# A fused attention and gated feed-forward kernel on one Trainium2 core: a second norm without its scaled sums, one more pair-added score half, and a new order

## The chip, the cores and the metric

The kernel runs on one core of one Trainium2 chip. The metric is the device time of one execution in microseconds (us), as the median of several runs. The engines of the core are named as in the profile: PE (matrix products), PEld (its weight loads), DVE (vector), ACT (scalar), POOL and SP, which here mostly issue DMAs.

## The reference, cut to what matters

x has 2048 rows of 512 numbers in bf16. H = 32 heads of 16 numbers; every position attends to W = 8 earlier positions, 2 apart.

```python
def _layernorm(x, eps=1e-5):
    return (x - mean(x)) / sqrt(var(x) + eps)

def _A_ref(x, wqkv, wo):                     # sliding, dilated attention
    q, k, v = split(x @ wqkv)                # 32 heads of 16
    idx = pos[:, None] - arange(8) * 2       # eight positions back, two apart
    logits = einsum("bhsd,bhswd->bhsw", q, k[idx]) * 16 ** -0.5   # masked where idx < 0
    return einsum("bhsw,bhswd->bhsd", softmax(logits), v[idx]) @ wo

def _B_ref(x, W_gate, W_up, W_down):         # 512 -> 1376 -> 512
    return (relu(x @ W_gate) * (x @ W_up)) @ W_down

h  = x + _A_ref(_layernorm(x), A_wqkv, A_wo)
h2 = h + _B_ref(_layernorm(h), B_W_gate, B_W_up, B_W_down)
```

The second norm is what the change touches first. The kernel does not divide h - mean by its standard deviation ahead of the two products: relu(a g) (a u) = a² relu(g) u for a positive a, so the rows go in centred only, and the factor 1 / (var + eps) is put on the output of the down product.

## The kernel before, in words

The rows are worked in four chunks of 512 (written tk, or "/0" to "/3" below), each of four blocks j of 128 rows. For a chunk: first norm (`xst`, `xag`, `xxn`), transposes (`xtp`), twelve q, k and v products of four matmuls each (`qkv`, for chunk 0's first six cut in parts `qka` to `qke`), and their copies out of PSUM on ACT (`qe`). The scores: for each half hf of the eight offsets DVE multiplies q by shifted k (`pr0`, `pr1`: two instructions of 128x4096 for a half, L638), PE sums over the 16 numbers of a head with a 0/1 matrix of 32 columns (`sc0`, `sc1`, L644), ACT takes exp (`ex`), DVE normalises (`es`, `am`), SP spreads each row over four partitions by DMA (`bd0S`, `bd1S`, L763), DVE multiplies by shifted v (`mu`, L795) and adds the eight products (`tree`, L798 and L832), where the first of three additions is an accumulating DMA that POOL issues (`ta`, L838). Then the output product (`wo`, L876), the residual sum on DVE (`rs`, L887), which also gives each row's sum `sm`, the second norm, transposes on PE (`htp`, chunk 0) or by DMA from SP (`htd`, L535, the other chunks), gate and up products (`mm`, L949; the last 96 of the 1376 columns as `mm5`, L916), copies and relu on ACT (`ue`, `ge`), the product gate times up on DVE (`gu`, L977, and `gu5`, L926), and the down product (`dn`, L1000) with its output step (`o`, `os`).

The second norm of a block before the change: DVE scales the row sum, mv = -sm / 512 (`hnm`, L452); ACT sums the squares of x + mv (`hsq`, L458); ACT makes 1 / (var + eps) as exp(-ln(...)) (`hrl`, `hre`, L479 and L486); DVE writes the centred rows x + mv (`hxn`, L512).

For chunk 3 both halves of the scores are pair-added: with (tk, hf) in `PRE`, DVE adds the second product tile to the first (`pa`, L682, one instruction of 128x4096), and PE sums 8 tiles instead of 16 (L689).

The order is no hand-written loop. Every step is an operation with an engine, a duration, dependences and buffers, and the list `RANK` gives each its place. `Plan.order` walks the operations strictly in the order of `RANK`, sets each at the earliest time its own cost table allows, and issues them in the order of these times. So every engine has one fixed sequence, and an engine waits at the first instruction whose input is not there.

At the start, SP and ACT issue the loads of x and of the four slices of the q and k weights (`wqk_sb`, L324 from ACT for slices 0 to 2, L339 from SP for slice 3). Parts `qka` and `qkd` of the first products need slices 0 and 1, part `qkb` needs slices 2 and 3.

Of the kernel before, what the change touches and what calls it, by code (L numbers as in the profile page):

```python
# [8 lines left out]
P = 128  # L9
BF16 = mybir.dt.bfloat16  # L10
F32 = mybir.dt.float32
I32 = mybir.dt.int32
ACT = mybir.ActivationFunctionType
# [188 lines left out]
def kernel(  # L202
# [11 lines left out]
    nc = tc.nc  # L214
# [11 lines left out]
    PRE = ((3,0),(3,1))  # L226
# [31 lines left out]
    eps_t = sb.tile([P, 1], F32, name="eps_t")  # L258
# [57 lines left out]
    def setup():  # L316
# [11 lines left out]
        nc.gpsimd.memset(eps_t[:], EPS)  # L328
# [108 lines left out]
    def layernorm(tk, src, dst_slots, pr, groups, on_act, residual=None):  # L437
# [7 lines left out]
        for grp in groups:  # L445
            ag, nms = [], {}
            gk = str(grp[0]) if len(groups) > 1 else ""
            lo, hi = grp[0], grp[-1] + 1
            for j in grp:
                if residual:  # L450
                    def f_nm(j=j):
                        V.tensor_scalar(out=mv.t[:, j, 0:1], in0=sm.t[:, j:j + 1], scalar1=-1.0 / D,  # L452
                                        scalar2=None, op0=ALU.mult)

                    h = src[j][1] if tk in RPE else None

                    def f_sq(j=j, h=h):
                        nc.scalar.activation(out=junk[:, j % 2, :], in_=h.t[:] if h else x_sm[:, tk * BPC + j, :],  # L458
                                             func=ACT.Square,
                                             bias=mv.t[:, j, 0:1], scale=1.0, accum_out=sq.t[:, j:j + 1])  # L460

                    a = nms[j] = add((ln + "nm" + gk, tk), "DVE", DSM, f_nm, [src[j][0]], pr, take=[mv], use=[sm], lat=DL)
                    ag.append(add((ln + "sq" + gk, tk), "ACT", 0.66 if h else 0.72, f_sq, [a], pr,
                                  take=[sq], use=[mv] + ([h] if h else []), lat=AL))
# [12 lines left out]
            def f_ln(lo=lo, hi=hi, sq=sq):  # L477
                if residual:
                    nc.scalar.activation(out=rs.t[:, lo:hi], in_=sq.t[:, lo:hi], func=ACT.Ln,  # L479
                                         bias=eps_t[:, 0:1], scale=1.0 / D)  # L480
                else:
                    nc.scalar.activation(out=rs.t[:, lo:hi], in_=mv.t[:, lo:hi, 1], func=ACT.Ln,
                                         bias=eps_t[:, 0:1], scale=1.0 / D if sq else 1.0)
# [23 lines left out]
            def f_xn(j, xn):  # L507
                x = x_sm[:, tk * BPC + j, :]
                if residual and on_act:
                    nc.scalar.activation(out=xn.t[:], in_=x, func=ACT.Identity, bias=mv.t[:, j, 0:1], scale=1.0)  # L510
                elif residual:
                    V.tensor_scalar(out=xn.t[:], in0=x, scalar1=mv.t[:, j, 0:1], scalar2=None, op0=ALU.add)  # L512
# [577 lines left out]
```

## Time and profile before

| | us |
|---|---|
| median of 3 runs | 192.77 (192.36 to 194.35) |
| the profiled execution | 193.22 |
| span of its trace, first to last instruction | 191.3 |
| PE busy, of the span | 185.3 (97%) |
| DVE busy | 149.6 (78%) |
| ACT busy | 115.2 (60%) |
| granted PE clock | 0.997 |

The span leaves out 1.9 us of the execution's own time. In the views below a row of a timeline begins with its start from the span's first instruction and its length, both in us; "x8" is a count, "A<-B" is output from input, and a bracket tells how long the engine sat idle ahead of it and what ended that. A row of a group of instructions ends with busy us, the mean ns of one, and the idle us in front of them.

### The profile page before, as it was taken

Reading aid. Unit: us, or ns where it says so; the run is one execution under the profiler, and the core shown is the slowest. Engines: PE = TensorE matmul, PEld = TensorE weight load, DVE = VectorE, ACT = ScalarE, POOL = GpSimd, SP = SyncE. Lnnn points to the kernel's source line nnn. Section 1 sums busy time; section 2 is a strip of 40 time slices with the busy share of each in tenths; the row PEclk is TensorE's granted clock in tenths of the full one; section 3 lists DMA queues with packets and bytes.
Section 4 is the critical chain, followed back from the end, with each engine's and each line's share of the span. In section 5 each row is a group of like instructions: output and inputs, shape, how many; then the busy total and the mean of one; then the engine's idle time right before and its main releaser. Section 6 shows DMA issues by size and latency. Waiting matters only on the chain.

```text
span 191.3 us, 3033 instructions
## 1 busy us (share of the span) xinstructions
PE 185.3 (97%) x1101; PEld 96.5 (50%) x1120; DVE 149.6 (78%) x246; ACT 115.2 (60%) x236; POOL 18.5 (10%) x34
## 2 busy tenths in 40 slices
PE   7899999999999999999999999999999999999993
PEld 7795555544455444644445544444446444445452
DVE  6899999999999999999999987999627503212632
ACT  2589999976748967753454875144855528517500
POOL 3000002500000042000055000042100000000000
PEclk9999999999999999999999999999999999999998
DMA  5998464992068589993479916779900460120302
GB/s 159 331 351 327 102 157 84 200 196 45 0 258 228 168 154 193 183 279 61 88 131 186 203 33 139 164 151 186 211 4 0 82 165 0 31 82 0 82 25 88
DMA packets 26718, 26.44 MB, mean 138 GB/s; under 512 B 12528, under 2 KB 22608, under 8 KB 26704
## 3 DMA queue, kind: packets, MB, share of 16 engines
q1 hardware_dynamic: 23248, 16.39, 30.9%
q0 software_dynamic: 2736, 8.91, 25.1%
q10 hardware_dynamic: 720, 0.95, 1.5%
q8 instruction: 9, 0.15, 0.3%
q14 instruction: 5, 0.04, 0.1%
HBM read 8.42 MB, written 2.10 MB: 55 GB/s over the span
## 4 chain that ended last, share of the span: by engine, by line
PE 94%; DMA 3%; issue 1%; ACTq 0%; DVE 0%
PE bank L949 36%; PE bank L587 22%; PE bank L1000 20%; PE bank L876 7%; DMA wqk_sb<-in_A_wqkv_dram 3%; PE bank L644 3%; PE bank L916 3%; PE bank L546 2%; PE bank L689 1%; PE bank L720 0%; ACTq L324 0%; ACTq L322 0%; DVE row L1008 0%
## 5 line engine op out<-in xcount | busy, mean ns | idle before, releaser
L949 PE MATMUL bank<-quad,wgu_sb 128*128 128x512 bf16 x311 | 72.1, 379 | 0.4
L949 PEld LDWEIGHTS <-wgu_sb 128*128 128x128 bf16 x320 | 30.9, 98 | 36.9 <-issue 1.7
L1000 PE MATMUL bank<-wd_sb,gT 128*128 128x512 bf16 (+3 forms) x195 | 39.6, 355 | 0.2
L956 ACT ACTIVATE gr<-bank 128x512 bf16<-128x512 f32 x40 | 23.2, 607 | 17.0 <-PE bank L949 13.0
L977 DVE TENSOR_TENSOR gT<-gr,up_sb 128x1024 bf16<-128x1024 bf16 x20 | 13.7, 688 | 23.5 <-ACT up_sb L953 20.3
L587 PE MATMUL bank<-quad,wqk_sb 128*128 128x512 bf16 (+2 forms) x171 | 30.0, 319 | 1.0 <-DMA wqk_sb<-in_A_wqkv_dram 0.7
L953 ACT CAST up_sb<-bank 128x512 bf16<-128x512 f32 x40 | 22.6, 594 | 10.5 <-PE bank L949 8.5
L1000 PEld LDWEIGHTS <-gT 128*128 128x128 bf16 (+1 forms) x198 | 18.5, 98 | 19.9
L638 DVE TENSOR_TENSOR big<-quad,kT 128x4096 bf16<-128x4096 bf16 x11 | 24.9, 2283 | 0.0
L587 PEld LDWEIGHTS <-wqk_sb 128*128 128x128 bf16 x176 | 16.9, 114 | 11.2 <-DMA wqk_sb<-in_A_wqkv_dram 0.9
L795 DVE TENSOR_TENSOR big<-big,vT 128x4096 bf16<-128x4096 bf16 x9 | 20.2, 2282 | 0.0
L458 ACT ACTIVATE junk<-x_sm,mv 128x512 bf16<-128x512 bf16 x16 | 11.7, 730 | 10.0 <-DVE mv L452 9.9
L587 PE MATMUL bank<-quad,wv_sb 128*128 128x512 bf16 x63 | 15.6, 379 | 0.1
L876 PE MATMUL bank<-wo_sb,quad 128*128 128x512 bf16 x63 | 15.2, 379 | 0.1
L838 POOL DMA_DIRECT2D big<-big x12 | 11.2, 1018 | 38.5 <-PE bank L587 29.4
L887 DVE SCALAR_TENSOR_TENSOR x_sm<-x_sm,bank 128x512 bf16<-128x512 bf16 x16 | 10.5, 680 | 3.7 <-PE bank L876 3.7
L798 DVE TENSOR_TENSOR big<-big 128x1024 bf16<-128x1024 bf16 (+2 forms) x18 | 11.5, 655 | 0.1
L1008 DVE SCALAR_TENSOR_TENSOR row<-bank,iv,x_sm 128x512 bf16<-128x512 f32 (+2 forms) x10 | 6.2, 640 | 6.8 <-PE bank L1000 6.8
L469 DVE BATCH_NORM_STATS2 st<-x_sm 128x6 f32<-128x512 bf16 x16 | 10.3, 681 | 1.2 <-DMA x_sm<-in_A_x_dram 1.2
L595 ACT CAST kT<-bank 128x512 bf16<-128x512 f32 x16 | 9.1, 592 | 2.8 <-DVE big L638 2.8
L595 ACT CAST quad<-bank 128x512 bf16<-128x512 f32 x16 | 9.4, 596 | 2.1 <-PE bank L587 1.9
L595 ACT CAST vT<-bank 128x512 bf16<-128x512 f32 x16 | 9.4, 596 | 2.0 <-PE bank L587 2.0
(79 smaller groups left out, 173.7 us busy)
## 6 DMA issues: line engine op xcount, KB each, us to landing
big<-big POOLq DMA_DIRECT2D x12, 512.0 KB, 5.7
big<-ex SPq DMA_DIRECT2D x32, 128.0 KB, 2.7
wqk_sb<-wqk_sb POOLq DMA_DIRECT2D x3, 512.0 KB, 4.5
wgu_sb<-in_B_W_gate_dram SPq DMA_DIRECT2D x1, 1376.0 KB, 11.2
wgu_sb<-in_B_W_up_dram SPq DMA_DIRECT2D x2, 688.0 KB, 4.7
wd_sb<-in_B_W_down_dram SPq DMA_DIRECT2D x2, 640.0 KB, 5.2
x_sm<-in_A_x_dram SPq DMA_DIRECT2D x2, 512.0 KB, 7.2
x_sm<-up_sb POOLq DMA_DIRECT2D x4, 256.0 KB, 5.1
```

Source lines behind the costliest of these rows:

```text
L458: nc.scalar.activation(out=junk[:, j % 2, :], in_=h.t[:] if h else x_sm[:, tk * BPC + j, :], func=ACT.Square, bias=mv.t[:, j, 0:1], scale= ...
L587: nc.tensor.matmul(mm.t[:, lo:hi], lhsT=wv_sb[:, dt, t:D:NT] if c == 2 else wqk_sb[:, dt, c * D + t:(c + 1) * D:NT], rhs=xnT.t[:, dt, lo:h ...
L595: nc.scalar.copy(out=o, in_=mm.t[:])
L638: V.tensor_tensor(out=pb.t[:].rearrange("p (t w) s -> p t w s", t=2), in0=q4, in1=k4, op=ALU.mult)
L795: V.tensor_tensor(out=mt.t[:], in0=ab.t[:], in1=v8, op=ALU.mult)
L798: V.tensor_tensor(out=mt.t[:, 0:n, :], in0=mt.t[:, 0:n, :], in1=mt.t[:, n:2 * n, :], op=ALU.add)
L876: nc.tensor.matmul(od.t[:], lhsT=OT.t[:, t, j * P:(j + 1) * P], rhs=wo_sb[:, t, :], start=(t == 0), stop=(t == NT - 1 and tk not in RPE))
L949: nc.tensor.matmul(mm.t[:fs, lo:hi], lhsT=wgu_sb[:, dt, g, ft * P: ft * P + fs], rhs=hnT.t[:, dt, lo:hi], start=(dt == 0), stop=(dt == NT ...
L953: nc.scalar.copy(out=ub.t[:fs, i, :], in_=um.t[:fs, :])
L956: nc.scalar.activation(out=gr.t[:fs, i, :], in_=gm.t[:fs, :], func=ACT.Relu)
L977: V.tensor_tensor(out=gt.t[:fs, 0:n, :], in0=gr.t[:fs, 0:n, :], in1=ub.t[:fs, 0:n, :], op=ALU.mult)
L1000: nc.tensor.matmul(od.t[:, c0:c1], lhsT=gts[ft].t[:fs, ft % 2, j * P:(j + 1) * P], rhs=wd_sb[:fs, ft, c0:c1], start=(ft == 0), stop=(ft == ...
```

## The change

The second norm works without `hnm`: instead of x - sum/512 it takes 512 x - sum, so the sum is used as it is. Squares, variance and centred rows grow by 512 or its square, and eps with them; the factor on the output divides it out. The pair addition is extended to the second half of chunk 2, `(2,1)`. `RANK` is a new list of 745 places in place of 760. `PRE2` is empty, so the branch for it makes nothing.

```diff
 RANK = [
...
-    21, 24, 26, 29, 33, 37, 36, 20, 22, 25, 27, 31, 35, 40, 39, 23, 28, 30, 32, 44,
+    21, 24, 26, 29, 33, 37, 36, 20, 22, 25, 27, 31, 35, 40, 43, 23, 28, 30, 32, 39,
...
-    PRE = ((3,0),(3,1))
+    PRE = ((2,1),(3,0),(3,1))
+    PRE2 = ()
...
-    eps_t = sb.tile([P, 1], F32, name="eps_t")
+    eps_t = sb.tile([P, 2], F32, name="eps_t")
...
-        nc.gpsimd.memset(eps_t[:], EPS)
+        nc.gpsimd.memset(eps_t[:, 0:1], EPS)
+        nc.gpsimd.memset(eps_t[:, 1:2], EPS * D * D)
...
-                    def f_nm(j=j):
-                        V.tensor_scalar(out=mv.t[:, j, 0:1], in0=sm.t[:, j:j + 1], scalar1=-1.0 / D,
-                                        scalar2=None, op0=ALU.mult)
-
...
                                              func=ACT.Square,
-                                             bias=mv.t[:, j, 0:1], scale=1.0, accum_out=sq.t[:, j:j + 1])
+                                             bias=sm.t[:, j:j + 1], scale=-float(D), accum_out=sq.t[:, j:j + 1])
...
                     nc.scalar.activation(out=rs.t[:, lo:hi], in_=sq.t[:, lo:hi], func=ACT.Ln,
-                                         bias=eps_t[:, 0:1], scale=1.0 / D)
+                                         bias=eps_t[:, 1:2], scale=1.0 / D)
...
                 elif residual:
-                    V.tensor_scalar(out=xn.t[:], in0=x, scalar1=mv.t[:, j, 0:1], scalar2=None, op0=ALU.add)
+                    V.tensor_scalar(out=xn.t[:], in0=x, scalar1=float(D), scalar2=sm.t[:, j:j + 1], op0=ALU.mult, op1=ALU.subtract)
...
-                d, u = ([nms[j]], [mv]) if residual else ([e], [nb, rs] if on_act else [mv, rs])
+                d, u = ([src[j][0]], [sm]) if residual else ([e], [nb, rs] if on_act else [mv, rs])
```

How the new list moves instructions shows at three places. In the rows, numbers behind a name tell buffers apart, and lines of the changed kernel are a few off those of before (L587 is L584, L546 is L543, L638 is L635, L682 is L679, L795 is L799, L926 is L930, L763 is L767, L308 is L309, L535 is L532, L935 is L939).

The first place is on PE at the start, around the first matmul that needs slice 2 of the q and k weights; it is the first row of 128x256, and the loads and matmuls of 128x128 on `wqk_sb` in front of it need slices 0 and 1 alone. `row_107` is the fourth block's normed rows, which PE transposes. Before:

```order
L546 LDWEIGHTS row_107
L546 MATMUL bank_140<-identity,row_107 128x128
L587 LDWEIGHTS wqk_sb
L587 MATMUL bank_144<-quad_79,wqk_sb 128x128
L587 LDWEIGHTS wqk_sb
L587 MATMUL bank_144<-quad_79,wqk_sb 128x128
L587 LDWEIGHTS wqk_sb
L587 MATMUL bank_144<-quad_79,wqk_sb 128x256
```

Now:

```order
L584 LDWEIGHTS wqk_sb
L584 MATMUL bank_145<-quad_79,wqk_sb 128x128
L584 LDWEIGHTS wqk_sb
L584 MATMUL bank_145<-quad_79,wqk_sb 128x128
L584 LDWEIGHTS wqk_sb
L584 MATMUL bank_145<-quad_79,wqk_sb 128x256
L584 LDWEIGHTS wqk_sb
L584 MATMUL bank_145<-quad_79,wqk_sb 128x256
L543 LDWEIGHTS row_107
L543 MATMUL bank_139<-identity,row_107 128x128
```

The fourth block's transposes and three of the parts that need only slices 0 and 1 went behind the first 128x256: from the first matmul on `wqk_sb` to the first of 128x256 there were 26 matmuls, of which the first is the one that starts on slice 0 alone, and there are 16 now.

The second place is on DVE in the middle of the program, where chunk 2's scores (L638, big from quad and kT) meet chunk 1's products with v (L795, from vT); L977 is a `gu` of chunk 0. Before:

```order
L638 TENSOR_TENSOR big_89<-quad_87,kT 128x4096
L638 TENSOR_TENSOR big_92<-quad_87,kT 128x4096
L795 TENSOR_TENSOR wqk_sb<-big_88,vT 128x4096
L795 TENSOR_TENSOR big_90<-big_88,vT 128x4096
L795 TENSOR_TENSOR big_91<-big_88,vT 128x4096
L977 TENSOR_TENSOR gT_93<-gr_111,up_sb_109 128x1024
```

Now:

```order
L635 TENSOR_TENSOR big_89<-quad_86,kT 128x4096
L635 TENSOR_TENSOR big_90<-quad_86,kT 128x4096
L930 TENSOR_TENSOR row_104<-gr_111,bank_141 128x2x96
L679 TENSOR_TENSOR big_91<-big_91,big_89 128x4096
L930 TENSOR_TENSOR row_104<-gr_111,bank_139 128x2x96
L799 TENSOR_TENSOR big_89<-big_92,vT 128x4096
L799 TENSOR_TENSOR big_88<-big_92,vT 128x4096
L799 TENSOR_TENSOR big_90<-big_92,vT 128x4096
L981 TENSOR_TENSOR gT_94<-gr_111,up_sb_110 128x1024
```

The new addition (L679, `pa1/2`) and chunk 0's two `gu5` (L930) now stand in front of chunk 1's products with v, and so in front of the accumulating DMAs behind them.

The third place is SP's sequence from chunk 1's second spread (the first L763) on; the rows of `wd_sb` load the down weights, L935 is chunk 0's transposed gate product, L535 on `quad_81` are chunk 1's four transposes. Before:

```order
L763 DMA big_88<-ex_100 128x1x512 x4
L308 DMA wd_sb<-in_B_W_down_dram 128x5x512
L763 DMA big_88<-ex_101 128x1x512 x4
L308 DMA wd_sb<-in_B_W_down_dram 128x5x512
L311 DMA wd_sb<-in_B_W_down_dram 96x512
L763 DMA big_88<-ex_102 128x1x512 x4
L535 DMA_TRANSPOSE quad_81<-row_107 128x4x128
L935 DMA_TRANSPOSE gT_97<-row_104 128x4x128
L535 DMA_TRANSPOSE quad_81<-row_105 128x4x128
```

Now:

```order
L767 DMA big_92<-ex_100 128x1x512 x4
L309 DMA wd_sb<-in_B_W_down_dram 128x5x512 x2
L312 DMA wd_sb<-in_B_W_down_dram 96x512
L939 DMA_TRANSPOSE gT_93<-row_104 128x4x128
L767 DMA wqk_sb<-ex_101 128x1x512 x4
L532 DMA_TRANSPOSE quad_81<-row_107 128x4x128
L532 DMA_TRANSPOSE quad_81<-row_106 128x4x128
L532 DMA_TRANSPOSE quad_81<-row_108 128x4x128
L532 DMA_TRANSPOSE quad_81<-row_104 128x4x128
L767 DMA wqk_sb<-ex_102 128x1x512 x4
```

The whole of the down weights is now issued right behind chunk 1's spreads, chunk 0's L939 stands ahead of chunk 2's first spread, and chunk 2's second spread stands behind chunk 1's four transposes.

More of the change, by code (lines that the diff above doesn't have):

```diff
@@ L445, in layernorm @@
         for grp in groups:
-            ag, nms = [], {}
+            ag = []
             gk = str(grp[0]) if len(groups) > 1 else ""
@@ L459, in f_sq @@
                                              func=ACT.Square,
-                                             bias=mv.t[:, j, 0:1], scale=1.0, accum_out=sq.t[:, j:j + 1])
-                    a = nms[j] = add((ln + "nm" + gk, tk), "DVE", DSM, f_nm, [src[j][0]], pr, take=[mv], use=[sm], lat=DL)
-                    ag.append(add((ln + "sq" + gk, tk), "ACT", 0.66 if h else 0.72, f_sq, [a], pr,
-                                  take=[sq], use=[mv] + ([h] if h else []), lat=AL))
+                                             bias=sm.t[:, j:j + 1], scale=-float(D), accum_out=sq.t[:, j:j + 1])
+                    ag.append(add((ln + "sq" + gk, tk), "ACT", 0.66 if h else 0.72, f_sq, [src[j][0]], pr,
+                                  take=[sq], use=[sm] + ([h] if h else []), lat=AL))
                 else:
@@ L479, in f_ln @@
                     nc.scalar.activation(out=rs.t[:, lo:hi], in_=sq.t[:, lo:hi], func=ACT.Ln,
-                                         bias=eps_t[:, 0:1], scale=1.0 / D)
+                                         bias=eps_t[:, 1:2], scale=1.0 / D)
                 else:
                     nc.scalar.activation(out=rs.t[:, lo:hi], in_=mv.t[:, lo:hi, 1], func=ACT.Ln,
-                                         bias=eps_t[:, 0:1], scale=1.0 / D if sq else 1.0)
+                                         bias=eps_t[:, 0:1], scale=1.0)
             def f_ex(lo=lo, hi=hi):
@@ L509, in f_xn @@
                 if residual and on_act:
-                    nc.scalar.activation(out=xn.t[:], in_=x, func=ACT.Identity, bias=mv.t[:, j, 0:1], scale=1.0)
+                    nc.scalar.activation(out=xn.t[:], in_=x, func=ACT.Identity, bias=sn.t[:, j:j + 1], scale=float(D))
                 elif residual:
-                    V.tensor_scalar(out=xn.t[:], in0=x, scalar1=mv.t[:, j, 0:1], scalar2=None, op0=ALU.add)
+                    V.tensor_scalar(out=xn.t[:], in0=x, scalar1=float(D), scalar2=sm.t[:, j:j + 1], op0=ALU.mult, op1=ALU.subtract)
                 elif on_act:
@@ L684, with f_pb, f_sc @@
                 a = add(("pa%d" % hf, tk), "DVE", D40, f_pa, [a for a, _, _ in prd], apr, use=[b for _, b, _ in prd], lat=DL)
-                def f_sc(sc=sc, pb=prd[0][1]):
-                    for u in range(2):
+                nu = 2
+                if (tk, hf) in PRE2:
+                    def f_pb(p0=prd[0][1]):
+                        V.tensor_tensor(out=p0.t[:, 0:4, :], in0=p0.t[:, 0:4, :], in1=p0.t[:, 4:8, :], op=ALU.add)
+                    a = add(("pb%d" % hf, tk), "DVE", D20, f_pb, [a], apr, use=[prd[0][1]], lat=DL)
+                    nu = 1
+                def f_sc(sc=sc, pb=prd[0][1], nu=nu):
+                    for u in range(nu):
                         for g in range(4):
@@ L690, in f_sc @@
                                              rhs=pb.t[:, 4 * u + g, :], start=(u == 0),
-                                             stop=(u == 1), tile_position=(0, g * HB))
-                scd = [add(("sc%d" % hf, tk), "PE", 2 * MM + SW, f_sc, [a], apr, take=[sc], use=[prd[0][1]], lat=PEL)]
+                                             stop=(u == nu - 1), tile_position=(0, g * HB))
+                scd = [add(("sc%d" % hf, tk), "PE", nu * MM + SW, f_sc, [a], apr, take=[sc], use=[prd[0][1]], lat=PEL)]
             elif tk in MERGE:
```

72 rows, old and new, of the table RANK are left out of this document.

## The prediction

> **What bounds the kernel now.** I read the page's busy times first, then the chain of waits, then busy time by stretch.
>
> ```profile
> PE 185.3 (97%) x1101; PEld 96.5 (50%) x1120; DVE 149.6 (78%) x246; ACT 115.2 (60%) x236; POOL 18.5 (10%) x34
> PE 94%; DMA 3%; issue 1%; ACTq 0%; DVE 0%
> 1.67 6.42 DMA wqk_sb<-in_A_wqkv_dram
> 8.09 0.05 issue
> 8.14 0.81 PE bank L587 x11
> ...
> 60.58 0.98 PE bank L644 x16
> ...
> 95.38 0.55 PE bank L689 x8
> ```
>
> The second row is the chain that ended last, by engine, and the rows below it are pieces of that chain: until 8.09 us it is the landing of a slice of the q and k weights, then PE, with nothing between its own pieces but 0.05 of issue now and then, up to the last output. So any PE work that goes is worth its full time, any new PE wait costs its full time, and work on other engines counts only where PE comes to wait for it. Busy time by stretch tells how near the others are:
>
> ```profile
> 44.00:87.00 43.00, 42.74 (x251) 20.80 (x254) 42.93 (x62) 29.16 (x59) 3.44 (x4) 1.00 0.65 164
> 140.00:188.00 48.00, 47.73 (x260) 24.32 (x263) 17.19 (x38) 21.12 (x47) 0.00 (x0) 1.00 0.19 50
> ```
>
> The columns are the stretch, its length, then busy us of PE, PEld, DVE, ACT, POOL, the granted clock, DMA share and GB/s. Between 44 and 87 us DVE is as full as PE (42.93 of 43.00), after 140 us it is mostly free. Two engines run side by side without a gap, so a DVE instruction too many there can reach PE, and one less gives nothing by itself.
>
> **The saved score products.** With `(2,1)` in `PRE`, `sc1/2` issues 8 matmuls instead of 16. The chain above has both forms: 0.98 for the 16 at 60.58, 0.55 for the 8 at 95.38. That is 0.98 - 0.55 = **-0.43 us** on PE.
>
> **The start.** Here the new order meets a weight load.
>
> ```profile
> wqk_sb<-in_A_wqkv_dram ACTq DMA_DIRECT2D x3, 256.0 KB, 6.4
> wqk_sb<-in_A_wqkv_dram SPq DMA_DIRECT2D x1, 256.0 KB, 5.7
> 3.74 0.33 SPq L339 DMA_DIRECT2D wqk_sb<-in_A_wqkv_dram  x1
> 9.39 0.22 PE bank L546 x4
> ```
>
> Slice 3 is issued from SP at 3.74 and lands 5.7 us later, at 9.44; the chain's 0.05 of issue puts its first matmul at 9.49 at the earliest. A matmul of 128 columns takes 0.22 / 4 = 0.055, one of 256 twice that. Before, the matmul at 8.14 is the second of the 26 in front of the first 128x256, so that one starts 25 x 0.055 later, at 9.52, and the next, the first on slice 3, at 9.63: later than 9.49, no wait. Now it is the second of 16: 8.14 + 15 x 0.055 = 8.97, and the first on slice 3 could start at 9.08. PE waits until 9.49: **+0.40 us**. Nothing behind it on PE can fill this, since PE runs its sequence in order. Bounds: 0, where slice 3 lands by 9.03, and 1.1, where it takes the 6.4 us of ACT's three slices.
>
> DVE's first products need copies of what these matmuls make, so DVE goes back by about the same 0.4, and the two engines stand to each other as before.
>
> **The removed scaling and the new form of the centred rows.** No cover is needed for a removal, but it must be seen what it is worth.
>
> ```profile
> L512 DVE TENSOR_SCALAR row<-x_sm,mv 128x512 bf16<-128x512 bf16 x16 | 5.1, 348 | 0.3
> L517 DVE TENSOR_SCALAR row<-x_sm,mv,rs 128x512 bf16<-128x512 bf16 x4 | 1.5, 402 | 0.0
> 55.47 0.32 DVE L452 TENSOR_SCALAR mv<-sm 128x1 f32<-128x1 f32 x4
> L682 DVE TENSOR_TENSOR big<-big,big 128x4096 bf16<-128x4096 bf16 x1 | 2.3, 2285 | 0.0
> ```
>
> A chunk's four `hnm` take 0.32 us together, so 16 free 1.3 us of DVE and none of PE. The centred rows go from one operation (348 ns) to two; the nearest row with two is L517 with 402, so 16 x 0.054 = 0.9 us more at most, nothing at least. The tier table of "VectorE: DVE Perf Modes" in the Trainium skill gives a bf16 tensor_scalar one rate, whatever its second operation; by that rule the extra is 0. The trace has 402 beside 348, where the slower one also reads two per-row scalars. I take 0.05 for each, 0.2 a chunk, and it does not reach PE (next part). ACT's squares keep their form, with another constant: 0, bounded by +-0.2 us a chunk on an engine 60% busy.
>
> **The pair addition and the order around it.** `pa1/2` is one instruction like L682, 2.28 us. With two `gu5` (L926) and one `gu` (L977) it now stands ahead of chunk 1's trees.
>
> ```profile
> L977 DVE TENSOR_TENSOR gT<-gr,up_sb 128x1024 bf16<-128x1024 bf16 x20 | 13.7, 688 | 23.5 <-ACT up_sb L953 20.3 <-ACT gr L956 2.3 <-PE bank L1000 0.9
> L926 DVE TENSOR_TENSOR row<-gr,bank 128x192 bf16<-128x192 bf16 x8 | 2.7, 348 | 0.5 <-ACT gr L922 0.5
> L747 DVE TENSOR_TENSOR ex<-ex,rec 128x512 bf16<-128x512 bf16 x6 | 2.4, 412 | 0.3 <-ACT rec L729 0.3
> 81.39 0.43 DVE L832 TENSOR_TENSOR quad<-big 128x512 bf16<-128x512 bf16 x1
> 82.03 3.34 PEld L876 LDWEIGHTS <-quad 128*128 128x128 bf16 x16
> 85.87 4.96 PE bank L1000 x23
> ```
>
> Chunk 1's output products (L876, from 82.03) need its last tree (L832, done 81.82). On DVE there stand ahead of that tree, now against before: +2.28 (`pa1/2`), +0.70 (two `gu5`), +0.69 (`gu1/0`), -0.32 (four `hnm`), -0.41 (one `am`), +0.2 (centred rows) = +3.1; with the start's 0.4 it is done at 85.3, or a little earlier, since neighbours overlap by some 0.08. On PE there stand ahead of the products the first eight matmuls each of `dn0/0` and `dn3/0`, which stood behind: 16 x 0.216 (4.96 / 23) = +3.46, and -0.43; with 0.4, 82.03 + 3.43 = 85.46. DVE is just ahead, as before: **0**. The bounds are 0 and +0.6, if DVE loses 0.8 us more than PE.
>
> Behind these products lies the second norm of chunk 1 with its transposes by DMA.
>
> ```profile
> 95.92 4.64 PE bank L949 x21
> 110.30 0.55 PE bank L689 x8
> 90.41 3.87 SPq L535 DMA_TRANSPOSE quad<-row  x3
> DMA to landing us min/median/max: 2.4/2.5/3.0
> DMA to landing us min/median/max: 2.6/2.7/2.8
> L887 DVE SCALAR_TENSOR_TENSOR x_sm<-x_sm,bank 128x512 bf16<-128x512 bf16 x16 | 10.5, 680 | 3.7 <-PE bank L876 3.7
> ```
>
> The two landing rows are those of the transposes and of a chunk 2 spread. PE had 95.92 - 85.87 = 10.1 us of other work between the last output product and the first `mm` of chunk 1; now 10.1 - 3.46 = 6.6. SP issues a transpose every 1.29 us (three in 3.87), and L935 no longer stands among the four. The second product ends at 85.46 + 1.73 = 87.2; `rs` (0.68) and centred rows (0.40) put the first transpose at 88.4, the last at 92.3, landed at 94.8. The work of PE ahead of that first `mm` is the same set as before, less 0.43 and with the 0.40: it comes there at 95.9. **0**, with 1.1 us to spare. Chunk 2's second spread now queues behind these four on SP: issued 93.6 to 96.2, landed at 98.3 to 98.9. DVE has one `am`, `pa0/3` and two `pr1/3` (7 us) ahead of the product that needs it and comes there at about 98.3: 0 to 0.6 us of DVE. PE's next need of this DVE work is `sc1/3`, at 110.30 before, now 3.9 earlier (three L949 products and two groups of L916 went behind it), at 106.4; DVE's `pa1/3` is done three instructions of 2.28 after 98.9, at 105.7. **0** again.
>
> **The end.** The last matmuls are now those of `dn5`, whose output leaves by ACT's queue, where before `dn4` was last, on SP.
>
> ```profile
> out_dram<-row ACTq DMA_DIRECT2D x1, 32.0 KB, 1.6
> out_dram<-row SPq DMA_DIRECT2D x1, 32.0 KB, 1.4
> ```
>
> 1.6 against 1.4: **+0.2 us**, bounds 0 and 0.3.
>
> **The sum**, on the profiled execution's 193.22 (span 191.3 and 1.9 around it): -0.43 + 0.40 + 0 + 0 + 0.2 = +0.17, 193.4. It lies 0.45 above the median of the runs, 192.77; the same change put on the median gives **192.9 us**. All places at their upper ends (1.1 + 0.6 + 0.3 - 0.43) give +1.6, 194.4; at their lower ends -0.43, 192.3.
>
> **The rivals.** Their times are put on the median.
>
> *Only the products count.* Slice 3 lands by 9.03 in most executions, and the end costs nothing: 192.77 - 0.43 = 192.3. For it: the landing is a single sample. Against it: 9.03 asks for 5.3 us where 5.7 was measured and ACT's three took 6.4.
>
> *The early down weights hold up the accumulating DMAs (slower).* The place is SP's and POOL's transfers at 63 to 83 us.
>
> ```profile
> 61.38 0.59 SPq L308 DMA_DIRECT2D wd_sb<-in_B_W_down_dram  x1
> 66.61 0.86 POOL L838 DMA_DIRECT2D wqk_sb<-wqk_sb  x1 [28.73 <-DVE wqk_sb L795]
> 74.16 0.86 POOL L838 DMA_DIRECT2D big<-big  x1 [2.28 <-DVE big L795]
> DMA to landing us min/median/max: 4.5/5.4/5.8
> DMA to landing us min/median/max: 4.5/5.0/5.4
> DMA to landing us min/median/max: 4.4/5.2/6.1
> ```
>
> The landing rows are those of chunk 1's four accumulations (issued from 66.61 to 74.16), of chunk 2's other spread, which went out right behind the second part of the down weights, and of the two parts themselves. That spread took 5.0 us against 2.7 without them. Now both parts go out one behind the other, at about 62.5 (the first at 61.38 before; one more score product stands ahead of chunk 1's second spread). On DVE the additions above, less the `gu` and the `am` that come later, put the first accumulation 2.9 + 0.4 later, at 69.9, the last 3.1 + 0.4, at 77.7. If the weights still move at 69.9, the delay d goes through all four, which follow each other closely. The last lands 5.5 after its issue, at 83.2 + d; DVE wants it one tree (1.1) before 85.3, at 84.2, and PE bears 0.2 beyond: from d = 1.2 on PE waits by d - 1.2. With d = 2.3, as the spread's, it is +1.1; with the 6.1 of a whole part +4.9; the middle, d = 4.2, gives +3.0 and, with the sum's +0.17, 195.9. Against it: the two parts at 4.4 and as much again would be done by 71.3, so d is 1.4 at the most, +0.2. The Trainium skill, "DMA: Bandwidth & Descriptors", section on issuing engines not being separate DMA queues, says that DMAs of all issuers share the same engines and interleave. The spread's 5.0 against 2.7 agrees.
>
> *Small hand-overs fail.* DVE is late at chunk 1's output products or the late spread goes through, or slice 3 takes ACT's 6.4: +0.4 to +1.4, 193.2 to 194.2.
>
> *The change does not do what it says:* the norm without `hnm` shortens a chain that PE never waits on, so its own effect is nil; it is part of every case above.
>
> **How the numbers follow.** A measurement of this kernel can tell about 1%, 1.9 us, from no change. Chances: the sum as above 0.50, only the products 0.17, small hand-overs 0.20, held accumulations 0.10 (a tenth of it within 1%), and 0.03 for a gain over 1% at the start or the end that no row here shows, since PE's own work falls by 0.43 alone. So faster 0.03, slower 0.09, same 0.88. The range 192.1 to 194.4 holds the first three cases and leaves out most of the fourth.
>
> **What would show it.** Right: L689 with 24 matmuls and L644 with 80; a wait of PE for `wqk_sb` of 0.3 to 0.5 at about 9.1; no PE wait over 0.2 between 10 and 188; the last landing on ACT's queue. Wrong: a PE wait at chunk 1's L876 or first L949, an accumulation landing over 6 us after its issue between 69 and 83, or the stretch from 44 to 87 with PE under 99%.

## The result, and the profile after

| | before | after |
|---|---|---|
| median, 22 runs of each on the same chips (us) | 192.63 | 193.82 |
| lowest and highest | 192.32, 194.35 | 192.56, 195.13 |
| the profiled execution | 193.22 | 193.91 |
| span of its trace | 191.3 | 191.0 |
| its time outside that span | 1.9 | 2.9 |

The ratio of the means, after to before, is 1.0054, 95% interval 1.0035 to 1.0074. The change makes the kernel about 1.0 us slower, where the prediction had +0.17. That is inside what it called no change (1%) and inside its range, but a small real loss. Run again later beside other kernels, the changed kernel gave 1.0034 (1.0014 to 1.0053), +0.65 us. The size is therefore 0.65 to 1.0 us.

The span of the traced execution tells the opposite of the median: 191.0 is less than 191.3. For one thing, the traced execution of the changed kernel spent 2.9 us outside its span, where the trace has no instruction, and that of before 1.9. Over its 22 runs the changed kernel spent 1.7 to 3.4 us there (six of them over 2.1), 2.03 on average; the kernel before spent 1.8 to 2.0, 1.87 on average, in its 90 runs beside the experiments below. By these averages about 0.16 us of the loss lies outside the span, and no run here tells why. The traced span is also among the shortest of the 22 (190.8 to 192.5, median 191.85).

For another, the two executions began differently, as PE's timelines show, first before, then after.

```profile
8.14 0.81 PE L587 MATMUL bank<-quad,wqk_sb 128*128 128x128 bf16 x11 [0.69 <-DMA wqk_sb<-in_A_wqkv_dram]
```

```profile
7.16 0.49 PE L584 MATMUL bank<-quad,wqk_sb 128*128 128x128 bf16 x6
```

Before, PE waited 0.69 us for weights ahead of its second q and k matmul and went on at 8.14. After, nothing held it there: its second matmul started at 7.16 + 0.055 = 7.21. To compare the two, take that matmul as the zero of a clock and the end of the last output product as its end. The last pieces of the two chains of waits (before, then after) give that end.

```profile
180.15 8.03 PE bank L1000 x58
```

```profile
182.89 4.88 PE bank L1004 x38
```

Before: 180.15 + 8.03 - 8.14 = 180.04. After: 182.89 + 4.88 - 7.21 = 180.56. On this clock the changed kernel is 0.52 longer, although its products are 0.43 shorter. So about 0.95 us of waiting is new, and the chain of waits tells where it sits. First its shares by engine, which were PE 94% before, then its pieces from 95 to 106 us.

```profile
PE 73%; DVE 16%; DMA 7%; issue 2%; SPq 1%; DVEq 0%
```

```profile
95.02 3.56 DMA wqk_sb<-ex
98.59 0.03 issue
98.62 0.05 DVEq L799
98.67 0.04 issue
98.71 4.49 DVE big L799 x2
103.20 2.21 DVE big L679
105.42 0.04 issue
105.46 0.61 PE bank L693 x8
```

This is chunk 2's second spread (its last DMA goes out at 95.02, lands at 98.59), two products on DVE that want it, the pair addition `pa1/3`, and PE's second score products of chunk 3. The timelines of PE and DVE give the waits at both ends.

```profile
98.71 4.49 DVE L799 TENSOR_TENSOR big<-wqk_sb,vT 128x4096 bf16<-128x4096 bf16 x2 [0.93 <-DMA wqk_sb<-ex]
```

```profile
103.82 1.24 PE L953 MATMUL bank<-quad,wgu_sb 128*128 128x512 bf16 x5
105.46 0.61 PE L693 MATMUL bank<-big,sel 128*32 128x512 bf16 x8 [0.40 <-DVE big L679]
```

DVE was idle for 0.93, PE for 0.40. The bracket counts from a modelled end. Counted from start to start it is a little more: five matmuls of 0.216 from 103.82 end at 104.90, a group of scores elsewhere starts 0.09 later than the next matmul would, so 105.46 is 0.47 late.

The second place is the first gate and up product of chunk 2. First PE's timeline, then SP's ahead of it.

```profile
126.64 1.03 PE L1004 MATMUL bank<-wd_sb,gT 96*128 96x512 bf16 x4
127.88 1.46 PE L953 MATMUL bank<-quad,wgu_sb 128*128 128x512 bf16 x6 [0.20 <-DMA quad<-row]
```

```profile
119.39 1.24 SPq L939 DMA_TRANSPOSE gT<-row  x1
120.73 1.21 SPq L532 DMA_TRANSPOSE quad<-row  x1
122.03 0.54 SPq L1036 DMA_DIRECT2D out_dram<-x_sm  x1
122.67 3.84 SPq L532 DMA_TRANSPOSE quad<-row  x3
```

PE could have gone on at 126.64 + 4 x 0.216 = 127.50 and started at 127.88, 0.20 by the bracket and 0.36 to 0.38 by the starts. SP issues without a pause from 119.39 to 126.51. Between the four transposes it issues a store of chunk 0's output (0.64 with its gap), and ahead of them the transpose of chunk 1's last gated columns (L939).

0.47 and 0.36 are 0.83 of the 0.95. The rest is in steps too small to name.

### The profile page after: what moved, and what is told of

Same layout as the page of the kernel before. It is cut to its first block, busy times and chain, and to the rows that moved or that the text cites. A ratio compares the mean times of both kernels' runs of the same rounds, so it can differ in the third digit from the quotient of the medians.

```text
span 191.0 us, 3017 instructions
## 1 busy us (share of the span) xinstructions
PE 184.9 (97%) x1093; PEld 96.1 (50%) x1112; DVE 150.4 (79%) x231; ACT 115.2 (60%) x236; POOL 18.5 (10%) x35
## 4 chain that ended last, share of the span: by engine, by line
PE 73%; DVE 16%; DMA 7%; issue 2%; SPq 1%; DVEq 0%
PE bank L953 23%; PE bank L584 21%; PE bank L1004 16%; DVE big L799 7%; PE bank L880 6%; PE bank L920 3%; DMA wd_sb<-in_B_W_down_dram 2%; PE bank L543 2%; PE bank L641 2%; DMA wqk_sb<-ex 2%; DMA x_sm<-in_A_x_dram 1%; DVE gT L981 1%; DMA quad<-row 1%; DVE big L679 1%; DVE big L635 1%
## 5 line engine op out<-in xcount | busy, mean ns | idle before, releaser
L1004 PE MATMUL bank<-wd_sb,gT 128*128 128x512 bf16 (+4 forms) x195 | 39.7, 355 | 0.2
L584 PE MATMUL bank<-quad,wqk_sb 128*128 128x512 bf16 (+2 forms) x172 | 29.8, 320 | 0.2
L635 DVE TENSOR_TENSOR big<-quad,kT 128x4096 bf16<-128x4096 bf16 x12 | 27.3, 2285 | 0.0
L584 PEld LDWEIGHTS <-wqk_sb 128*128 128x128 bf16 x176 | 16.9, 113 | 10.5 <-issue 0.4
L842 POOL DMA_DIRECT2D big<-big x14 | 12.6, 936 | 79.0 <-DVE big L799 44.4
L456 ACT ACTIVATE junk<-x_sm,sm 128x512 bf16<-128x512 bf16 x16 | 11.6, 729 | 8.7 <-DVE x_sm L891 8.7
L584 PE MATMUL bank<-quad,wv_sb 128*128 128x512 bf16 x62 | 15.7, 379 | 0.2
L799 DVE TENSOR_TENSOR big<-big,vT 128x4096 bf16<-128x4096 bf16 x7 | 15.7, 2283 | 0.0
L880 PE MATMUL bank<-wo_sb,quad 128*128 128x512 bf16 x63 | 14.4, 379 | 0.1
L802 DVE TENSOR_TENSOR big<-big 128x1024 bf16<-128x1024 bf16 (+2 forms) x20 | 12.9, 658 | 0.0
L880 PEld LDWEIGHTS <-quad 128*128 128x128 bf16 x64 | 6.2, 98 | 7.7 <-DVE quad L806 0.4
```

The source lines that it names most:

```text
L584: nc.tensor.matmul(mm.t[:, lo:hi], lhsT=wv_sb[:, dt, t:D:NT] if c == 2 else wqk_sb[:, dt, c * D + t:(c + 1) * D:NT], rhs=xnT.t[:, dt, lo:h ...
L635: V.tensor_tensor(out=pb.t[:].rearrange("p (t w) s -> p t w s", t=2), in0=q4, in1=k4, op=ALU.mult)
L799: V.tensor_tensor(out=mt.t[:], in0=ab.t[:], in1=v8, op=ALU.mult)
L802: V.tensor_tensor(out=mt.t[:, 0:n, :], in0=mt.t[:, 0:n, :], in1=mt.t[:, n:2 * n, :], op=ALU.add)
L842: nc.gpsimd.dma_start(mt.t[:, 0:4, :], mt.t[:, 4:8, :], accum_op=ALU.add)
L880: nc.tensor.matmul(od.t[:], lhsT=OT.t[:, t, j * P:(j + 1) * P], rhs=wo_sb[:, t, :], start=(t == 0), stop=(t == NT - 1 and tk not in RPE))
```

## The experiments

Theories, as the expectations name them. S+C: the loss is chunk 2's two hand-overs (C) and a start that is more exposed to late weights (S). S: the start alone. C: chunk 2 alone. V: the pair addition's 2.28 us make DVE too late.

The medians of the kernel before lie between 192.56 and 192.86 in these comparisons. Line numbers are those of the kernel after, unless the text says otherwise. A table at the end of this section puts the traces side by side.

**The second spread ahead of chunk 1's transposes.** The instruction order on DVE and SP:

```diff
 L751 TENSOR_TENSOR ex_101<-ex_101,rec_103 128x512
+L751 TENSOR_TENSOR ex_102<-ex_102,rec_103 128x512
 L802 TENSOR_TENSOR big_90<-big_90 128x1024
...
 L767 DMA wqk_sb<-ex_101 128x1x512 x4
+L767 DMA wqk_sb<-ex_102 128x1x512 x4
 L532 DMA_TRANSPOSE quad_81<-row_107 128x4x128
...
-L767 DMA wqk_sb<-ex_102 128x1x512 x4
```

> The changed kernel, with one VectorE product (the weights' scaling of chunk 2's second half) moved from behind the four centred rows of chunk 1 to right behind its twin of the first half, so that the four DMAs of the second spread of chunk 2 are issued on SP ahead of chunk 1's four transposes, not behind them. Theory S+C: the spread lands about 10 us earlier, VectorE's idle 0.92 us before its first product with it goes, and so PE's 0.47 at the second score products of chunk 3; part of the 0.36 at chunk 2's first gate and up products goes too, as VectorE is earlier there. 193.0 to 193.4, ratio 1.002 to 1.004. A cost that could take some of it back: SP's four issues (2.5 us) run until 87 and could hold up the first transpose by up to 0.4. Rival S: 193.8, the wait is gone in the trace and the time stays. Rival V: PE's wait at the scores is VectorE's own work and stays.

Measured: 1.0002 (0.9974 to 1.0030). DVE goes on to its products without idle time and PE to the scores likewise; the wait at chunk 2's gate and up products is gone as well. In exchange PE waits 0.15 at chunk 1's output products (their last tree stands 0.41 further back on DVE). The trace is as S+C had it; the ratio lies under its 1.002 to 1.004, and the interval reaches into that range. S and V fall, for the wait was neither covered nor DVE's own work.

**The store behind chunk 2's transposes.**

```diff
 L532 DMA_TRANSPOSE quad_85<-row_106 128x4x128
-L1036 DMA out_dram<-x_sm 128x2x512
 L532 DMA_TRANSPOSE quad_85<-row_108 128x4x128
 L532 DMA_TRANSPOSE quad_85<-row_104 128x4x128
 L532 DMA_TRANSPOSE quad_85<-row_105 128x4x128
+L1036 DMA out_dram<-x_sm 128x2x512
```

> The changed kernel, with the output store of one pair of chunk 0's rows (0.64 us of SP's queue) moved from between chunk 2's four transposes to behind them. Theory S+C: the last transpose goes out at 124.6, not 125.29, and lands at 127.1, before PE wants it at 127.3: the 0.36 at chunk 2's first gate and up products goes, 0.47 at the scores stays: 193.5, ratio 1.0035 to 1.0045. Rivals S and V: 193.8.

Measured: 1.0018 (0.9993 to 1.0044). SP's and PE's timelines of this kernel:

```profile
121.55 5.14 SPq L532 DMA_TRANSPOSE quad<-row  x4
126.78 0.54 SPq L1036 DMA_DIRECT2D out_dram<-x_sm  x1
```

```profile
125.66 2.55 PE L1004 MATMUL bank<-wd_sb,gT 128*128 128x512 bf16 x11
128.08 1.24 PE L953 MATMUL bank<-quad,wgu_sb 128*128 128x512 bf16 x5
```

The four transposes now go out in 5.14 and PE has no bracket at 128.08. The other wait stays (0.41 at the scores). The trace is as S+C expected; the ratio fell further than 0.36 us would take it, and its interval holds the expected ratio too. By itself this trace proves little: a second one of the changed kernel, with the store in its old place, has almost no wait there either (below).

**Why the spread was late: POOL's output accumulation in the middle of it.** In the changed kernel POOL issues two accumulating DMAs onto the residual rows (L1033, 256 KB each) at 94.42 and 97.65, the first of them while the spread is on its way (92.64 to 98.59).

```diff
+L1033 DMA x_sm<-up_sb   (oa1/0)
 L1033 DMA x_sm<-up_sb   (oa3/0)
-L1033 DMA x_sm<-up_sb   (oa1/0)
...
-    up_s = slots(2, [P, 2, CS], BF16, "up_sb")
+    up_s = slots(3, [P, 2, CS], BF16, "up_sb")
```

> The changed kernel, with POOL's first accumulating DMA of chunk 0's output rows (it was issued at 94.42, in the middle of chunk 2's second spread) behind the second one (97.65), and a third buffer for its source so that ScalarE waits for nothing; room for that buffer comes from one ex buffer fewer and a smaller scratch tile for the squares. The order on all other engines is unchanged. Theory C, with the transfer's share as the reason: the spread lands 2.6 to 2.8 after its last issue, at 97.6 to 98.0 and not at 98.59, VectorE's idle time of 0.92 falls under 0.3 and PE's 0.47 at the scores goes: ratio 1.002 to 1.004. Rival Q (the place in SP's queue alone makes it late): the spread lands as late as before and PE waits 0.4 to 0.5: 1.005.

Measured: 1.0012 (0.9991 to 1.0034). The spread's landing times, first of the changed kernel, then of this one:

```profile
L767 SPq DMA_DIRECT2D wqk_sb<-ex x4: 543/555/618, 92.6 to 95.0; - x4
DMA to landing us min/median/max: 2.5/2.7/3.6
```

```profile
L767 SPq DMA_DIRECT2D wqk_sb<-ex x4: 543/555/614, 92.8 to 95.2; - x4
DMA to landing us min/median/max: 2.5/2.6/2.8
```

SP issues the four in the same time. What differs is the landing of the last of them, which DVE waits for: 3.6 in the changed kernel, 2.6 here (the 2.8 is another's). The timelines of POOL, DVE and PE in this kernel:

```profile
97.96 1.75 POOL L1033 DMA_DIRECT2D x_sm<-up_sb  x2 [20.40 <-ACT up_sb L1010]
```

```profile
97.89 4.49 DVE L799 TENSOR_TENSOR big<-wqk_sb,vT 128x4096 bf16<-128x4096 bf16 x2
```

```profile
103.78 1.46 PE L953 MATMUL bank<-quad,wgu_sb 128*128 128x512 bf16 x6
105.17 0.61 PE L693 MATMUL bank<-big,sel 128*32 128x512 bf16 x8
```

No idle time on DVE, none on PE. The wait at chunk 2's gate and up products went too, with the store still among the transposes: SP's first of them goes out at 119.88 instead of 120.73, as DVE is 0.8 earlier. So the second loss hangs on the first as well as on the store. The ratio is again under the expected 1.002 to 1.004, and the interval reaches into it. Rival Q falls: the place in the queue puts the spread beside the accumulation, and alone it would not have made it late. The section of the Trainium skill's "DMA: Bandwidth & Descriptors" on issuing engines not being separate DMA queues says that transfers of all issuers share the same engines and interleave; 3.6 against 2.6 agrees. An accumulation is not the only thing that lengthens a spread: in the first experiment, where eight went out in a row and none of POOL's DMAs was on its way, the slowest took 3.6 as well.

**The changed kernel without the pair addition.** `(2,1)` is taken out of `PRE` again, the order is left as it is.

> The changed kernel without the pair addition for chunk 2: its second half of score products is again 16 matmuls on the unadded products, all else in the new order. Theory C: both waits of chunk 2 come from what is queued on SP, and stay at 0.3 to 0.5 each; PE has 0.43 more: ratio 1.006 to 1.0085. Rival V (the 2.28 us that the addition puts on VectorE make it late in chunk 2): the waits go, 1.002 to 1.004.

**The changed kernel again.**

> The changed kernel itself, once more, beside the others on the same chip. Every theory: ratio 1.0035 to 1.0074, and the two waits of chunk 2 in the trace, 0.47 at the scores and 0.36 at the gate and up products, if they belong to the order and not to one execution; the waits of the start may differ.

Measured: 1.0057 (1.0030 to 1.0083) without the addition, 1.0034 (1.0014 to 1.0053) with it. PE's brackets at the scores of chunk 3, first without, then with the addition:

```profile
106.55 0.61 PE L693 MATMUL bank<-big,sel 128*32 128x512 bf16 x8 [0.51 <-DVE big L679]
```

```profile
105.36 0.61 PE L693 MATMUL bank<-big,sel 128*32 128x512 bf16 x8 [0.53 <-DVE big L679]
```

DVE has 2.28 us less to do and PE waits the same. V falls. Without the addition the ratio is a little under C's 1.006 to 1.0085, which its interval reaches into. The second wait was 0.27 without the addition and too small for a bracket with it (0.14 from start to start), so this one varies from execution to execution, from nearly nothing to 0.36. The difference of the ratios, 0.0023, is 0.44 us, the size that the prediction gave the eight saved matmuls (0.43); the intervals overlap, so it is a hint, not a measurement.

**Each part alone in the order of before.** First the second norm's edit, with `RANK` of before less its 16 places for `hnm`.

> The kernel before, in its own order, with the second norm's edit alone (no scaled row sums, centred rows at 512 times their value by two operations on VectorE); the score products are left as they were. Every theory here: no PE wait hangs on these rows, ratio 0.999 to 1.001. Rival N (the two-operation rows are slower by more than the 0.05 us taken, and come late at the transposes): 1.002 or more, with the rows' mean duration over 0.40 us.

Then the pair addition.

```diff
-    PRE = ((3,0),(3,1))
+    PRE = ((2,1),(3,0),(3,1))
```

> The kernel before with the pair addition of chunk 2's second half alone: the addition stands right behind the two products that it adds, and the two groups of chunk 2's score matmuls stand four and five products of L949 further back, nothing else moves. Theory S+C, by the prediction's sum: 2.28 us more of VectorE stand ahead of chunk 1's last tree with nothing put in front of it on PE, which comes there 0.43 earlier and had 0.2 to spare, so PE waits 2.2 to 2.5 at chunk 1's output products and the time grows by 1.8 to 2.1: ratio 1.009 to 1.011. Rival P (VectorE has slack there, the products alone count): 0.998. Between the two, 1.003, if later slack takes half of it back.

Measured: 1.0003 (0.9983 to 1.0022) for the norm. The groups by line of its trace have its centred rows at the time of the old ones (345 against 348 ns), and of the kernel after at 350:

```profile
L509 DVE TENSOR_SCALAR row<-x_sm,sm 128x512 bf16<-128x512 bf16 x16 | 4.9, 345 | 0.1
```

```profile
L509 DVE TENSOR_SCALAR row<-x_sm,sm 128x512 bf16<-128x512 bf16 x16 | 5.5, 350 | 0.4
```

For the pair addition: 1.0117 (1.0090 to 1.0143), 2.25 us slower. PE's timeline of it (in this kernel L950 are the gate and up products, L721 the softmax sums, L877 the output products):

```profile
60.81 3.61 PE L950 MATMUL bank<-quad,wgu_sb 128*128 128x512 bf16 x15 [0.77 <-ACT quad L563]
73.60 0.39 PE L721 MATMUL bank<-row,same 128*128 128x512 bf16 x1 [0.53 <-DVE row L736]
83.75 3.63 PE L877 MATMUL bank<-wo_sb,quad 128*128 128x512 bf16 x16 [0.43 <-ACT gr L957]
```

The size is what S+C expected and a little more, and the reason is DVE, as S+C had it. DVE's timeline has no pause from 55.87 to the end of chunk 1's last tree, whose row is

```profile
83.27 0.42 DVE L833 TENSOR_TENSOR quad<-big 128x512 bf16<-128x512 bf16 x1
```

It is done at 83.69, and the output products start at 83.75. Counted from the second q and k matmul (8.14 before, 7.58 here, less 0.12 of waiting at the start), that tree ends 2.3 us later than before. S+C expected one PE wait of over 2 there. There are three instead, but the first two take nothing more: since DVE did not pause, PE would have stood that much longer at the tree without them. (The third bracket names ACT, whose copy was done at 83.72, beside the tree.) So rival P falls: DVE has no slack for the addition in the old order. In the new one the addition costs nothing that these runs can tell (1.0057 without it, 1.0034 with it).

**The start.** First everything up to the first exp in the order of before.

> The changed kernel, with everything up to the first exp of chunk 0's scores put back in the order of the kernel before (26 small q and k matmuls, not 16, ahead of the first 128x256 one). Theory S+C (start and chunk 2): of the +1.0 us (193.82 against 192.63) some 0.4 to 0.5 is PE's wait for slices of the q and k weights, which the shorter lead-in makes longer on average (the profiled execution had none), and 0.83 is chunk 2's two hand-overs (0.47 at the second score products of chunk 3, 0.36 at the first gate and up products of chunk 2), against -0.43 for the saved products. It expects 193.3 to 193.4, ratio 1.004, with both waits of chunk 2 still in the trace. Rival S (start alone): the waits in chunk 2 are covered by slack elsewhere, all of the loss is at the start: 192.6 or less, ratio 1.000. Rival V (VectorE is overloaded by the pair additions): no change, 193.8.

Measured: 1.0111 (1.0069 to 1.0153), slower. The joint between the two orders made waits of its own (PE's timeline):

```profile
21.93 1.02 PE L584 MATMUL bank<-quad,wv_sb 128*128 128x512 bf16 x4 [0.22 <-ACT quad L559]
33.46 1.03 PE L584 MATMUL bank<-quad,wv_sb 128*128 128x512 bf16 x4 [0.56 <-DMA quad<-row]
```

The second of them is not the joint's alone: at the same products PE waits 0.28 in the run with the store moved and 0.20 in that with two moves (below), and under 0.1 in the changed kernel. So the run says nothing on the start, and the same holds for the run that joins it to the two moves:

> The three moves of the runs before in one kernel (start order of before, second spread ahead of chunk 1's transposes, store behind chunk 2's). Theory S+C: only the saved products and what is left of the start remain: 192.2 to 192.6, ratio 0.998 to 1.000, and no PE wait over 0.2 us after 10 us. Rival S: 192.6, as with the start alone. Rival V: VectorE is still late in chunk 2, 193.4 or more.

Measured: 1.0052 (1.0025 to 1.0079), with the same two waits (0.22 and 0.45) and chunk 2 free of waits.

**Two moves together, and with the old lead-in.** Both moves, with the scaling behind chunk 1's last tree; then the same with 26 small matmuls again ahead of the first 128x256; then both moves with the scaling where the first experiment had it.

> The changed kernel with two moves: the scaling of chunk 2's second half on VectorE goes right behind chunk 1's last tree and its four DMAs go ahead of chunk 1's transposes on SP, and the store of chunk 0's rows goes behind chunk 2's transposes. Theory S+C: both waits of chunk 2 go (0.83), and the 0.15 at chunk 1's output products that the earlier place of the scaling cost goes too; left are -0.43 for the products and what the start costs on average: ratio 0.998 to 1.000, 192.3 to 192.7 where before is at 192.7. Theory C' (chunk 2 is all there is, the start costs nothing on average): ratio 0.9978. Rival V (VectorE too full): 1.003 or more.

> The run before, and in the start's PE sequence the four transposes of the fourth row tile and six small matmuls of the q and k products that want other slices go ahead of the first ones on the slice issued last: 26 small matmuls ahead of the first 128x256 one, not 16, all else left alone. Theory S+C: PE waits less for that slice, 0.2 to 0.4 on average: ratio 0.996 to 0.998, and in the trace no wait for that slice; a wait for the fourth row tile, if its rows land late, is as long as before. Theory C': the same as the run before, within 0.1 per cent.

> The changed kernel with the scaling of chunk 2's second half at the place of the run e2_spread (behind its twin, so that SP's four issues are over before chunk 1's first transpose is ready) and the store of chunk 0's rows behind chunk 2's transposes. Theory C (the loss after 10 us is SP's queue in chunk 2): no wait at the scores, none at chunk 2's gate and up products, 0.15 at chunk 1's output products and under 0.1 at chunk 1's first gate and up products: -0.43 + 0.2 = -0.23 after 10 us, and with 0.2 to 0.4 for the start a ratio of 1.000 to 1.001; 0.9985 if the start costs nothing on average. Rival: the moves only push the loss elsewhere, 1.004 or more as in the changed kernel.

Measured: 1.0015 (0.9990 to 1.0040), 1.0018 (0.9990 to 1.0046) and 1.0033 (1.0013 to 1.0053). All three are above what was expected. In all three SP's eight spread issues ran into the first transpose of chunk 1, and PE waited at its first gate and up products; the rows are of the third, SP's timeline, then PE's:

```profile
82.52 6.09 SPq L767 DMA_DIRECT2D wqk_sb<-ex  x8
88.70 5.87 SPq L532 DMA_TRANSPOSE quad<-row  x4
```

```profile
95.82 1.46 PE L953 MATMUL bank<-quad,wgu_sb 128*128 128x512 bf16 x6 [0.53 <-DMA quad<-row]
```

In the first experiment the same eight issues took 5.11 and PE's wait there stayed under 0.1; in the three runs one of the eight took 1.2 to 1.5 us, in the first none over 0.6. That order has no room on SP.

On slice 3, two of the executions with the short lead-in show it in PE's timeline (the store behind the transposes, then the two moves together):

```profile
8.53 0.27 PE L584 MATMUL bank<-quad,wqk_sb 128*128 128x256 bf16 x1 [0.32 <-DMA wqk_sb<-in_A_wqkv_dram]
```

```profile
9.32 0.27 PE L584 MATMUL bank<-quad,wqk_sb 128*128 128x256 bf16 x1 [0.27 <-DMA wqk_sb<-in_A_wqkv_dram]
```

Counted between starts, four of the eight traces with the short lead-in have a wait for slice 3 (0.49, 0.43, 0.19, 0.18), and none of the six with the long one. The mean over the eight is 0.16. But the time didn't follow: the run with the long lead-in was no faster than the same kernel without it, its interval leaves out the 0.996 to 0.998 that S+C expected, and in its trace PE waits 0.99 for the transposes' third row tile instead.

All traces, by PE's clock: from the second q and k matmul to the end of the last product. Waits between them ahead of 10 us, counted from start to start, are taken off, so that the column shows what happens after the start:

| kernel | ratio to before | start's waits | PE's clock without them |
|---|---|---|---|
| before | 1 | 0 | 180.0 |
| norm alone | 1.0003 | 0 | 179.9 |
| pair addition alone | 1.0117 | 0.12 | 182.0 |
| after | 1.0054 | 0 | 180.6 |
| after, again | 1.0034 | 0 | 180.3 |
| after without the addition | 1.0057 | 0.44 | 181.0 |
| after, accumulation moved | 1.0012 | 0.19 | 179.6 |
| after, spread moved | 1.0002 | 1.20 | 179.8 |
| after, store moved | 1.0018 | 0.49 | 180.4 |
| after, two moves | 1.0015 | 0.43 | 180.4 |
| the same, long lead-in | 1.0018 | 1.30 | 180.0 |
| two moves, scaling as first | 1.0033 | 0.62 | 180.2 |
| after, start of before | 1.0111 | 0.09 | 181.3 |
| the same with both moves | 1.0052 | 0 | 180.4 |

179.6 with the accumulation moved is the 180.0 of before less 0.43: with both hand-overs gone the saved products appear in full. No version beat the kernel before for certain: the best two with the new order are 1.0002 and 1.0012, and their intervals hold 1. The time outside the span is now and then longer in the kernels with the new order: over 2.1 us in 22 of 133 runs, against 1 of 108 (2.15) with the order of before.

## Why the prediction was right in kind and wrong in size

- **The saved products, -0.43:** right. L693 has 24 matmuls and L641 has 80, and the 0.43 shows in full once nothing waits.
- **The start, +0.40 for slice 3:** the mechanism is there in half of the traces, the size was too large: 0.16 on average of eight traces. The sum took one landing (9.44) from one execution, and that one was late. The rows give the landings of all four slices, before and then after:

```profile
DMA to landing us min/median/max: 4.0/6.1/6.6
```

```profile
DMA to landing us min/median/max: 3.6/4.5/5.2
```

  Whether the short lead-in costs more than 0.16, by late row tiles or the other slices, stays open; the runs made for it didn't settle it.
- **The norm, 0:** right, and the 0.05 for each row with two operations was 0.00 (350 and 345 against 348 ns). The tier table of "VectorE: DVE Perf Modes" in the Trainium skill lists one rate for a bf16 tensor_scalar and sets a second operation apart nowhere; the trace agrees. So the row with 402 was slower for another reason, perhaps its second per-row scalar, which wasn't tried.
- **Chunk 1's output products, 0:** right, no wait in the trace, and the pair addition without the new order shows what stood on it (2.25 us).
- **Chunk 1's first gate and up products, 0:** right.
- **The second scores of chunk 3, 0 again:** this step failed. It had the queue right (the spread goes out behind the four transposes) but took a landing of 2.6 to 2.8 from a spread of the kernel before, beside which an accumulation was only ending (issued at 74.16, it landed 5.5 later). Here one was issued right ahead of the last of the four, and that one took 3.6. The prediction had `pa1/3` done at 105.7 and PE there at 106.4, 0.7 to spare. This execution began 0.93 earlier (7.21 for 8.14) and without the 0.40 at the start, which makes the two 104.4 and 105.1. Measured, PE was there at 104.99, as forecast, and `pa1/3` was done at 105.41, 1.0 late: 0.9 of it is the landing (3.6 for the 2.7 used), 0.1 the issue. PE's bracket there is 0.40 to 0.53 in every trace that kept this order.
- **Chunk 2's first gate and up products:** no step of the prediction was about them. The new order puts a store and another transpose into SP's queue there, and DVE's late start is handed on: 0.1 to 0.4. This is the second failure: the queue was followed past one chunk and not past the next.
- **The end, +0.2:** the last output does leave by ACT's queue, in the trace at no cost. Whether the longer time outside the span hangs on it wasn't tried.

```profile
out_dram<-row SPq DMA_DIRECT2D x1, 32.0 KB, 1.5
out_dram<-row ACTq DMA_DIRECT2D x1, 32.0 KB, 1.5
```

- **The rivals:** held accumulations did not come. Chunk 1's four landed in 4.5, 5.4 and at most 6.0 us, against 4.5, 5.4 and 5.8 before; 6 was the sign that the prediction had set. "Small hand-overs fail", 193.2 to 194.2, with a chance of 0.20, is what happened: 193.82 lies in it, and the late spread that "goes through" was one of the three places that it named. That 193.82 also lies inside the range is in part luck: the 0.40 put at the start and the 0.83 put at nothing are different losses, and the range was wide enough for either.

With the measured terms the sum is -0.43 + 0.16 + 0.70 to 0.95 (PE's clock of the two traces of the changed kernel, less 179.6) = +0.4 to +0.7, for +0.65 and +1.0 measured. The rest is 0.2 to 0.4. In the first comparison 0.16 of it lies outside the span, in the second nothing (1.83 against 1.88 on average); the 0.2 that is left in both belongs to no row. The kernel with the long lead-in restored has a rest of that size too (0.35 by its ratio, none by PE's clock), so it isn't shown to be the start's.

## What to carry to other kernels

A landing time is the price of a transfer together with what else moved at that time: before using a row of the trace, look what the other queues issue between its issue and its landing in the new order. Where an engine's queue is moved past a step, follow that queue until it is next empty, through the next chunk too; the second loss sat 22 us behind the first. And where PE has no idle time, look at the hand-overs with the least slack first: here 0.7 us of it was gone when one DMA took 0.9 longer, and PE waited 0.4 to 0.5 for it, as much as the change had saved.

## What the runs showed of the hardware

One accumulating DMA of 256 KB, issued 0.6 us ahead of the last of four 128 KB spreads, lengthened the landing of that one from 2.6 to 3.6 us and left their median as it was (2.6 and 2.7). The loads of the first weights land after a median of 4.3 to 6.1 us in different executions of kernels that issue them at nearly the same times, and with them the start of the products moves by up to 1 us (7.1 to 8.1 for the second matmul). A difference of some tenths between two kernels can't be read from two spans.
